# Attention scores with the bias on TensorE, attention steps in pairs, and offsets in a planner's order

## The chip, the cores and the metric

The kernel runs on one core of a Trainium2 chip. The metric is device microseconds from launch to end. A profile of one execution gives the time of every instruction on the engines: TensorE (PE, matmuls; PEld its weight loads), VectorE (DVE), ScalarE (ACT), GpSimd (POOL) and SyncE (SP), which issues the DMAs.

## The reference

For 4 batches, 8 heads, 768 positions and a head size of 64, each query attends to a window of its neighbours and to 24 block summaries of all keys. The result goes through a gated feed-forward network, whose weights come as float64.

```
k_sum = k.reshape(B, H, nb, 32, D).max(axis=3)       # block keys: maximum
v_sum = v.reshape(B, H, nb, 32, D).mean(axis=3)      # block values: mean
scores_l = where(|pos_q - pos_k| < 16, scale * q @ k.T, -1e9)
scores_s = scale * q @ k_sum.T + log(32)
a = exp(s - max(s));  a = a / (sum(a) + 1e-9)        # s: both kinds of scores side by side
x = a @ [v, v_sum]                                   # 3072 tokens x 512
g = x @ w_gate;  out = ((g * sigmoid(g)) * (x @ w_val)) @ w_out
```

## The kernel before, in words

**Attention.** A unit (k, u) is half a batch (384 tokens; k = 2 * batch + half) and a pair of heads u. There are 32 units, 8 to a batch. The tokens of a unit are cut into six groups of 64. A group's scores are 96 window columns and 24 block columns, 120 in all, and three groups share a PSUM bank. The steps of a unit are:

- SC (`a_scores`, L457): 24 matmuls of 64 x 64 weights by 120 columns, into two banks. The 120 columns come from a tile `kw` that holds, for each group, its window of keys and a copy of the block keys. For the first half of batch 0 `kw` is copied from the keys (`a_copy_windows`, L434), for all others it is loaded again from memory in 384-byte pieces (`a_load_windows`, L424). `join` (L449) puts the block keys behind them.
- `ttr` (`most`, L482): on VectorE, six instructions that take a bank's scores, add a bias (the mask and log 32), write them to SBUF and keep the minimum of the negated scores. Then six exps on ScalarE (L500), `eps` (L515), `rcp` (L518) and `nrm` (L521).
- PP0 and PP1 (L529): six transposes on TensorE, copied out as `pt`.
- XO (`a_out`, L550): 24 matmuls into one bank, then copied out by `xh` and `xl` (batch 0) or `xf`.
- The block values: `FV` in batch 0; in later batches a reduction `vpool`, a single transpose `PV` (`a_turn_values`, L651) and a copy `vs`.

**Network.** All of it runs as float32r with each operand split into a high and a low part, three products for one. `w_first` (L801) decodes a float64 weight tile on VectorE and ScalarE (`abs`, `clamp`, `shift`, `sign`, `low`), splits it (`hi`, `lo`), forms sums of quarters and stores them for the later batches. `o_first` (L839) does the same for each of the 12 tiles of the output weight, 512 wide. In batch 0 `u_plain` (L866) multiplies directly, 12 matmuls to a bank. In batches 1 to 3 `u_seven` (L911) uses seven products of quarters instead of eight, P1, P7, P5, P6, P2, P4, P3, in four banks, with VectorE adding them up (`vv`, `u2`, `c21`, `c12`, `c22`). `down` (L947) multiplies by the output weight and adds to `part`.

**Where the work stands in time.** While the network of one batch runs, the attention of the next is put between its steps (`units`, L1118). Batch 0's attention comes first, with batch 0's network behind it.

**What sets the order.** Nothing is ordered by hand. Every step is entered in a plan with an estimated time for each engine that could do it (`cost`, L74). `run` (L203) plays the plan through as a list scheduler: TensorE has a main line (the network) and a side line (attention), and takes of the two heads the one that can start first; other engines take the waiting step with the smallest due time. `order` (L170) does this three times, each time with due times from the round before, and sorts the steps by their planned start. The program is written in that order, so the order on each engine is fixed, and an instruction that waits holds up all that stand behind it on its engine. Where the plan has TensorE idle in the first 110 us, `warm_up` (L996) puts filler matmuls on a tile `warm`.

**Banks.** Of PSUM's eight banks three are a ring "t" (attention) and five a ring "m" (network; also some of batch 0's attention).

Of the kernel before, what the change touches and what calls it, by code (L numbers as in the profile page):

```python
# [18 lines left out]
DM = H * D  # L19
# [21 lines left out]

F64_LO = float(np.uint32(0x38000000).view(np.float32))
# [3 lines left out]
def score_bias() -> np.ndarray:  # L46

    m = np.zeros((P, 3, KC), np.float32)
    second, r = np.divmod(np.arange(P)[:, None], QT)
    c = np.arange(KW)[None, :]  # L50
    out = np.abs(r + WIN - c) >= WIN

    for v, edge in enumerate(((c < WIN) & (second == 0), c < 0, (c >= WIN + QT) & (second == 1))):
        m[:, v, :KW] = np.where(out | edge, np.float32(-1e9 / SCALE), np.float32(0))
    m[:, :, KW:] = np.float32(math.log(BLK) / SCALE)
    return m
# [46 lines left out]
class Step:  # L103
    def __init__(self, name, engines, do, n):
        self.name, self.engines, self.do, self.n = name, engines, do, n
        self.after, self.next = {}, []
        self.engine = self.start = self.end = None


class Plan:  # L110
# [26 lines left out]
    def add(self, name, engines, do, reads=(), writes=(), table=None, port=None):  # L137
# [3 lines left out]
        step.port = port  # L141
# [24 lines left out]
WAIT = 1.0  # L166
HOLD = 0.2


def order(steps):  # L170
# [13 lines left out]
    for _ in range(3):  # L184
# [18 lines left out]
def run(steps, line, late):  # L203
# [7 lines left out]
    table, place = None, [0, 0]  # L211
# [23 lines left out]
    while n:  # L235
        best = None
        for e, waiting in ready.items():
            if not waiting:
                continue
            if e == PE:  # L240
# [5 lines left out]
                s = min(heads, key=lambda s: (when(s), not s.side))  # L246
                pick = (when(s), 0, s)
# [35 lines left out]
        took = s.engines[e]  # L283
        if s.table and s.table != table:
            table, took = s.table, took + TABLE
# [5 lines left out]
        if e == PE:  # L291
            place[s.side] += 1
        n -= 1
# [4 lines left out]
def body(ctx, tc, qP, kP, vT, vP, wgv, wo, bias, ident, mean, out):  # L298
# [43 lines left out]
    def bank(which, name):  # L342
        return buf("psum", which, [P, 512], name, bufs={"t": 3, "m": 5}[which])
# [37 lines left out]
    bias_sb = buf("cst", "bias", [P, 3, KC], "bias_sb")  # L381
    id_sb = buf("cst", "id", [P, P], "id_sb")
    mean_sb = buf("pro", "mean", [P, NV, NB], "mean_sb")
# [9 lines left out]
    def a_keys(k, u):  # L393
        b = k // HALVES
        pool = "pro" if b == 0 and u % 2 else "att"
# [20 lines left out]
    def window_tile(k, u):  # L416
        if (k, u) not in KWD:
            pro = k == 0
            KWD[k, u] = buf(
                "pro" if pro else "att", f"kw{u}" if pro else "kw", [P, NT, KC], f"kw_{k}_{u}", bufs=1 if pro else 2  # L420
            )
        return KWD[k, u]
# [11 lines left out]
    def a_copy_windows(u):  # L434
        kt, kw = KT[0, u], window_tile(0, u)
        add_copy(
            f"winA({u})", (DVE, POOL, ACT), NT * QT, lambda: make(kw)[:, :, :QT],
            lambda: make(kt)[:, :TOK].rearrange("p (n j) -> p n j", j=QT), (kt,), ((kw, "w"),),
        )

        def tails():
            t = make(kt)
            return bass.AP(t.tensor, t.offset + QT, [t.ap[0], [QT, NT], [1, KW - QT]])

        add_copy(
            f"winB({u})", (DVE, POOL, ACT), NT * (KW - QT), lambda: make(kw)[:, :, QT:KW], tails, (kt,), ((kw, "v"),)
        )

# [7 lines left out]

    def a_scores(k, u):  # L457
        q, kw = Q[k, u], KWD[k, u]
# [3 lines left out]
        def do(e):  # L462
            warm_up(make(sc[0]))
            for i in range(NT):
                c, s = divmod(i, 2)
                qs = slice(i * QT, (i + 1) * QT)
                for h in range(2):
                    hs = slice(h * D, (h + 1) * D)
                    nc.tensor.matmul(  # L469
                        make(sc[h])[s * QT : (s + 1) * QT, c * KC : (c + 1) * KC], make(q)[hs, qs], make(kw)[hs, i, :],  # L470
                        start=True, stop=True,
                    )

        plan.add(f"SC({k},{u})", {PE: 0.95}, do, (q, kw), sc)

    def a_softmax(k, u):
# [20 lines left out]
        def half_exp(g):  # L497
            for c in range(NT // 2):
                i = g * NT // 2 + c
                nc.scalar.activation(  # L500
                    out=make(p)[:, i, :],
                    in_=make(p)[:, i, :],
                    func=AF.Exp,
                    scale=-1.0,
                    bias=make(nm)[:, i : i + 1],
                    accum_out=make(sm)[:, i : i + 1],
                )

        for g in range(2):
            plan.add(f"ttr{g}({k},{u})", {DVE: 1.1}, lambda e, g=g: most(g), (sc[g], bias_sb), ((p, g), (nm, g)))  # L510
        for g in range(2):
            plan.add(f"exp{g}({k},{u})", {ACT: 1.75}, lambda e, g=g: half_exp(g), ((nm, g),), ((p, g), (sm, g)), table="exp")
        plan.add(
            f"eps({k},{u})", {DVE: 0.18},
            lambda e: nc.vector.tensor_scalar(out=make(sm), in0=make(sm), scalar1=1e-9, scalar2=None, op0=ALU.add),  # L515
            (), (sm,),
        )
# [11 lines left out]
    def a_transposes(k, u):  # L529
        p = PR[k, u]  # L530
        if k == 0 and u % 2:
            pt = buf("pro", "pt", [KC, 2, TOK], f"pt_{k}_{u}")
        else:
            pt = buf("att", "pt", [KC, 2, TOK], f"pt_{k}_{u}")
        PT[k, u] = pt
        for g in range(2):
            pp = bank("m" if k == 0 else "t", f"pp{g}_{k}_{u}")

            def turn(e, g=g, pp=pp):
                warm_up(make(pp))  # L540
                for c in range(NT // 2):
                    nc.tensor.transpose(make(pp)[:KC, c * P : (c + 1) * P], make(p)[:, g * NT // 2 + c, :], make(id_sb))  # L542

            plan.add(f"PP{g}({k},{u})", {PE: 0.38}, turn, (p, id_sb), (pp,))
# [3 lines left out]
            )  # L548

    def a_out(k, u):  # L550
# [24 lines left out]
        plan.add(f"XO({k},{u})", {PE: 1.0}, do, reads, (xo,))  # L575
# [75 lines left out]
    def a_turn_values(b, u):  # L651
        vr = VR[b, u]
        pv = bank("t", f"pv_{b}_{u}")

        def do(e):
            nc.tensor.transpose(make(pv)[:NB, :P], make(vr), make(id_sb))

        plan.add(f"PV({b},{u})", {PE: 0.12}, do, (vr, id_sb), (pv,))
        if b not in VS:
# [4 lines left out]
            lambda e: nc.scalar.mul(make(vs)[KW:, u * P : (u + 1) * P], make(pv)[:NB, :P], 1.0 / BLK),  # L664
            (pv,), ((vs, u),),
# [173 lines left out]
    def o_first(j):  # L839
        raw = buf("wts", f"o{j}", [P, 2 * DM], f"raw_o{j}", I32)  # L840
        add_dma(f"raw_o{j}", P * DM * 8, lambda: make(raw), lambda: wo[j].bitcast(I32), (), (raw,))
        m = buf("dec", "mo", [P, DM], f"m_o{j}", bufs=2)
        decode(f"o{j}", raw, m, DM)
        w = O[j] = buf("wts", f"o{j}", [P, 2, DM], f"o{j}", F32R)
        split(f"o{j}", w, m, DM)
# [43 lines left out]
    def product(b, j, name, weight, xname, acc, first, last):  # L889
# [6 lines left out]
        def do(e):  # L896
            t = make(acc)
            warm_up(t)
# [12 lines left out]
    def u_seven(b, j):  # L911
        tmp = lambda name: buf("tmp", name, [P, TOK], f"{name}_{b}_{j}", room="tmp")
        p1, p7, p5, p6 = (bank("m", f"{x}_{b}_{j}") for x in ("p1", "p7", "p5", "p6"))
        of = lambda x: lambda: make(x)[:, :TOK]
        full = lambda x: lambda: make(x)
        product(b, j, "P1", "A11", "B11", p1, True, False)
        s1 = tmp("s1")
        add_copy(f"s1({b},{j})", (ACT, DVE), TOK, full(s1), of(p1), (p1,), (s1,), kind="evict")
        product(b, j, "P7", "S3", "T3", p7, True, False)
        s7 = tmp("s7")  # L920
        add_copy(f"s7({b},{j})", (ACT, DVE), TOK, full(s7), of(p7), (p7,), (s7,), kind="evict")
        product(b, j, "P5", "S1", "T1", p5, True, False)
        v = tmp("v")
        add_tt(f"vv({b},{j})", (DVE,), TOK, full(v), of(p5), full(s7), ALU.add, (p5, s7), (v,))
        product(b, j, "P6", "S2", "T2", p6, True, True)
# [21 lines left out]
    def down(b, g, t, spread):  # L947
# [6 lines left out]
        def piece(n):  # L954
            todo = pieces[n]

            def do(e):
                ps = make(acc)
                warm_up(ps)
                for j in todo:  # L960
                    ah, al = (make(x)[:, cs] for x in HH[b, j, hf])
                    wh, wl = (make(O[j])[:, x] for x in range(2))
# [5 lines left out]
            reads = sum(([*HH[b, j, hf], O[j]] for j in todo), [])  # L968
# [40 lines left out]
    def before_scores(k, u):  # L1009
# [4 lines left out]
        a_load_windows(k, u)  # L1014
# [4 lines left out]
        a_load_values(k, u)  # L1019
        a_join(k, u)  # L1020

    @aside
    def scores(k, u):
        before_scores(k, u)
        a_scores(k, u)
# [3 lines left out]
    def turned(k, u):  # L1029
        b, hf = divmod(k, HALVES)  # L1030
        if b and hf == 0:
            a_turn_values(b, u)
        a_values(k, u)
        a_transposes(k, u)

    @aside
    def result(k, u):
# [3 lines left out]
        else:  # L1041
            a_keep(k, u)

# [11 lines left out]
    def prepare(u):  # L1055
# [3 lines left out]
        a_copy_windows(u)  # L1059
        a_join(0, u)  # L1060

    for u in (1, 3):
        prepare(u)
        if u == 1:
            load_const(bias_sb, bias, P * 3 * KC * 4)
# [4 lines left out]
    load_const(id_sb, ident, P * P * 4)  # L1070
    load_first_values(0)

# [18 lines left out]
    plan.mark("late", "pro", lambda: (close_pool("pro"), open_pool("late", reuse_waits="tile")))  # L1091
# [9 lines left out]
    scores(1, 3)  # L1101
    for j in range(3):
# [15 lines left out]
    def units(b, at, gap, slack=SLACK):  # L1118
        plan.slack = slack
        for i in range(NP * HALVES):  # L1120
            k, u = b * HALVES + i // NP, i % NP
            todo.append((at + (i * gap / 2 if i < 2 else (i - 1) * gap), 2, lambda k=k, u=u: scores(k, u)))
            todo.append((at + (i + 0.55) * gap, 0, lambda k=k, u=u: turned(k, u)))
            todo.append((at + (i + 1) * gap, 1, lambda k=k, u=u: result(k, u)))
        todo.sort(key=lambda x: x[:2])
# [3 lines left out]
    def catch_up():  # L1129
        while todo and todo[0][0] <= clock[0]:  # L1130
            todo.pop(0)[2]()
# [7 lines left out]
    units(1, 0.0, 10.0, 1.5)  # L1139
# [12 lines left out]
    while todo:  # L1152
        todo.pop(0)[2]()
    for b in range(1, B):
        x_operands(b)
        clock[0] = 0.0
        if b + 1 < B:
            units(b + 1, 4.0, 14.5)
# [6 lines left out]
        while todo:  # L1165
            todo.pop(0)[2]()
# [56 lines left out]
```

## Time and profile before

| what | us |
|---|---|
| three runs | 696.02, 697.10, 697.63; median 697.1 |
| the profiled execution | 695.64 |
| its span, first to last instruction | 693.8 |
| TensorE busy | 676.6 (98%), 4918 matmuls |
| VectorE busy | 543.0 (78%) |
| ScalarE busy | 350.2 (50%) |
| GpSimd busy | 107.8 (16%) |

The span is what the profile sees of the execution; 1.8 us lie around it. Shares are of the whole span. They are averages over stretches with different limits, so a stretch has to be read by itself. Matmuls overlap in the pipeline: a matmul's own duration is longer than the distance to the next start, and it is that distance that counts.

### The profile page before, as it was taken

What the parts mean: (1) busy time and instruction counts of PE and PEld (TensorE: products, weight loads), DVE (VectorE), ACT (ScalarE), POOL (GpSimd) and SP (SyncE); (2) the same over time, 40 slices, a digit from 0 to 9 for tenths busy, and PEclk for the clock granted to TensorE, in tenths of its full rate; (3) what the DMA queues carried; (4) which work ended last, traced back from release to release, by engine and by line L of the source; (5) the groups of instructions that cost most, each with busy time, mean ns of one, the idle gap of its engine ahead of it and who ended that gap; (6) DMA issues with size and microseconds to landing.
All of it is one profiled execution on the core that took longest, in us unless ns stands there. A gap on an engine that the chain in (4) does not pass through costs nothing.

```text
span 693.8 us, 13084 instructions
## 1 busy us (share of the span) xinstructions
PE 676.6 (98%) x4918; PEld 612.9 (88%) x4918; DVE 543.0 (78%) x1296; ACT 350.2 (50%) x826; POOL 107.8 (16%) x115
## 2 busy tenths in 40 slices
PE   9797999999999999999999999999999999999997
PEld 8586899899799898989989898989989898989896
DVE  5889999989999898796878875696758862646464
ACT  4676655757666285655634375653734423212120
POOL 2344203031331320320101120000000200000000
PEclk9999999999999999999999999999999999999999
DMA  9999766766657698795847675583625553535322
GB/s 318 317 336 336 245 234 240 244 209 224 220 156 265 228 325 277 236 355 171 267 160 237 237 264 181 152 257 90 231 82 203 195 207 123 208 111 201 119 106 92
DMA packets 73327, 150.15 MB, mean 216 GB/s; under 512 B 25968, under 2 KB 48176, under 8 KB 67120
## 3 DMA queue, kind: packets, MB, share of 16 engines
q1 hardware_dynamic: 73264, 149.32, 63.4%
q8 instruction: 39, 0.64, 0.4%
q14 instruction: 24, 0.20, 0.1%
HBM read 114.70 MB, written 34.60 MB: 215 GB/s over the span
## 4 chain that ended last, share of the span: by engine, by line
PE 91%; DVE 5%; DMA 2%; ACT 1%; issue 1%; SPq 0%; ACTq 0%
PE p L904 39%; PE acc L964 28%; PE g L881 7%; PE v L881 7%; PE sc L469 3%; PE xo L573 3%; PE pp L542 2%; DMA q<-in_qP 2%; PE sc L999 1%; PE dummy L1006 1%; DVE w L354 1%; DVE pt L351 0%; ACT m_w L766 0%; DVE part L354 0%; DVE m_w L770 0%
## 5 line engine op out<-in xcount | busy, mean ns | idle before, releaser
L964 PE MATMUL acc<-o,hh 128*128 128x512 f32 x576 | 182.6, 398 | 0.0
L964 PEld LDWEIGHTS acc<-o,hh 128*128 128x128 f32 x576 | 104.7, 188 | 22.6 <-issue 1.4
L904 PE MATMUL p<-xh_T,s 128*128 128x384 f32 x432 | 120.2, 340 | 0.0
L964 PE MATMUL acc<-o,hl 128*128 128x512 f32 x288 | 112.8, 392 | 0.0
L904 PE MATMUL p<-xh_B,wa 128*128 128x384 f32 x288 | 86.8, 342 | 0.0
L500 ACT ACTIVATE p<-p,nm 128x120 f32<-128x120 f32 x192 | 73.5, 385 | 20.6 <-DVE nm L486 20.2
L904 PEld LDWEIGHTS p<-xh_T,s 128*128 128x128 f32 x432 | 78.9, 188 | 1.4 <-issue 0.3
L904 PE MATMUL p<-xl_T,s 128*128 128x384 f32 x216 | 72.4, 335 | 0.0
L354 DVE TENSOR_TENSOR part<-acc,part 128x512 f32<-128x512 f32 x72 | 48.5, 685 | 23.2 <-PE acc L964 22.8
L964 PEld LDWEIGHTS acc<-o,hl 128*128 128x128 f32 x288 | 54.1, 188 | 12.0 <-DVE hl L354 0.2
L881 PE MATMUL g<-xh_B,w 128*128 128x384 f32 x192 | 55.6, 350 | 5.0 <-DVE w L354 5.0
L354 DVE TENSOR_TENSOR c<-p,u 128x384 f32<-128x384 f32 x72 | 39.7, 553 | 22.7 <-PE p L904 22.5
L349 ACT COPY s<-p 128x384 f32<-128x384 f32 x52 | 24.9, 478 | 59.9 <-PE p L904 59.7
L349 ACT CAST hh<-a 128x384 fp32r<-128x384 f32 x53 | 27.1, 514 | 54.9 <-DVE a L354 53.8
L904 PEld LDWEIGHTS p<-xh_B,wa 128*128 128x128 f32 x288 | 53.1, 188 | 1.6 <-issue 1.0
L881 PE MATMUL v<-xh_B,w 128*128 128x384 f32 x192 | 53.8, 341 | 0.0
L354 DVE TENSOR_TENSOR hl<-a,hh 128x384 fp32r<-128x384 f32 x89 | 51.2, 578 | 2.9 <-ACT hh L349 0.5
L486 DVE CUSTOM_DVE_ANT_0 p<-sc,bias_sb 128x120 f32<-128x120 f32 x192 | 41.8, 275 | 10.0 <-PE sc L469 9.6
L904 PE MATMUL p<-xl_B,wa 128*128 128x384 f32 x144 | 48.3, 335 | 0.0
L354 DVE TENSOR_TENSOR v<-p,s 128x384 f32<-128x384 f32 x36 | 20.0, 557 | 34.0 <-PE p L904 33.3
L904 PE MATMUL p<-xh_T,wa 128*128 128x384 f32 x144 | 42.7, 337 | 0.0
L904 PE MATMUL p<-xh_B,s 128*128 128x384 f32 x144 | 42.5, 335 | 0.0
(124 smaller groups left out, 1365.0 us busy)
## 6 DMA issues: line engine op xcount, KB each, us to landing
wa<-wa SPq DMA_DIRECT2D x36, 768.0 KB, 4.3
s<-ss SPq DMA_DIRECT2D x24, 1024.0 KB, 7.5
raw_w<-in_wgv SPq DMA_DIRECT2D x12, 1024.0 KB, 6.2
ss<-s SPq DMA_DIRECT2D x12, 1024.0 KB, 4.9
wa<-w SPq DMA_DIRECT2D x12, 768.0 KB, 4.3
kw<-in_kP SPq DMA_DIRECT2D x28, 288.0 KB, 5.2
vw<-in_vP SPq DMA_DIRECT2D x28, 288.0 KB, 5.0
kt<-in_kP SPq DMA_DIRECT2D x16, 400.0 KB, 5.4
```

Of the source, the lines that this page charges most:

```text
L349: nc.scalar.copy(out, in_)
L354: vector[e].tensor_tensor(out=out, in0=a, in1=b, op=op)
L469: nc.tensor.matmul(make(sc[h])[s * QT : (s + 1) * QT, c * KC : (c + 1) * KC], make(q)[hs, qs], make(kw)[hs, i, :], start=True, stop=True,)
L486: nc.vector.tensor_tensor_reduce(out=make(p)[:, i, :], in0=make(sc[g])[:, c * KC : (c + 1) * KC], in1=make(bias_sb)[:, 0 if n == 0 else 2 ...
L500: nc.scalar.activation(out=make(p)[:, i, :], in_=make(p)[:, i, :], func=AF.Exp, scale=-1.0, bias=make(nm)[:, i : i + 1], accum_out=make(sm ...
L542: nc.tensor.transpose(make(pp)[:KC, c * P : (c + 1) * P], make(p)[:, g * NT // 2 + c, :], make(id_sb))
L573: nc.tensor.matmul(ps[hs, qs], v, make(pt)[:, h, qs], start=True, stop=True)
L881: nc.tensor.matmul(t[:, :TOK], a, x, start=u == 0 and n == 0, stop=u == NP - 1 and n == 2)
L904: nc.tensor.matmul(t[:, :TOK], a, x, start=first and kk == 0 and n == 0, stop=kk == 1 and n == 2, skip_group_check=not first,)
L964: nc.tensor.matmul(ps, a, w, start=j == js[0] and m == 0, stop=j == js[-1] and m == 2)
L999: nc.tensor.matmul(ps[:, TOK:], make(warm), make(warm), start=True, stop=True)
L1006: nc.tensor.matmul(make(first)[:, :P], make(warm), make(warm), start=True, stop=True)
```

## The change

1. **Bias on TensorE for batch 0** (k below 2). The bias, split into parts that float32r holds exactly, is a new input `parts`. SC of these units ends with 8 more matmuls of the identity by the bias, which add it in the bank. `ttr` gives way to one maximum over a bank (`max`) and a scaling of three numbers (`scl`). The exps read the bank and not SBUF. The mask's number becomes -2**33.
2. **Keys read in place for batch 0.** SC reads the 96 window columns from the keys' tile and the 24 block columns from `ks`, in two matmuls where there was one. The copies, the window loads and the joins of these 8 units go.
3. **Attention steps in pairs.** From batch 1 on `units` enters SC, SC; then PP of both; then XO, XO and the next SC, SC as a `burst`. Steps of a burst share the dependencies of its first, and `run` takes the next one of a burst if it can start within JOIN (0.35 us). Planned costs of SC and XO are changed, with extra time on a switch between kinds (`mode`).
4. **Banks** 4 and 4 for 3 and 5.
5. **Output weight in pairs**: `o_first` decodes two tiles at once, 1024 wide.
6. `PV` joins PP0 as a fourth transpose into the same bank. `u_seven` does P6 first from its second tile on, and `a_values` comes after the transposes.
7. **Exps one by one** in the plan where there were two steps of three; `eps` can go to ScalarE or GpSimd.
8. **Offsets.** `nudge` adds to the due times of 212 named steps a number from a table, or sets a slack, or pins the engine (13 to ScalarE, 24 to VectorE, 21 to GpSimd); then `run` plays the plan once more.

The diff, cut to its core:

```
+NUDGES = """
+kt(0,1) -60.2; id_sb -72.2; vr(1) -12.4; kt(0,0) +8.2; kt(0,2) +20.3; pool(0,2) +97.4; vn(0) +23.7; bias_sb +35.4
+scl1(0,3) -50.5 d; exp2(0,3) -108.4; exp5(0,3) -90; SC(0,0) s0.8; exp0(0,0) -54.7; exp1(0,0) -34.7; exp3(0,0) +137.8
...
+raw_w0 +14.7; low_w0 +106.4; wa0 +51.7; odd2(0) -51 p; val1(0) -42.4 p; odd2(2) -53.7 a; val1(2) -102.9 p
...
+exp3(1,3) +5.5; exp4(1,3) +47.8; eps(1,3) +121.7 p; raw_o0 +23.5; low_o0 +69.4; lo_o0 +58.3 d; raw_o2 +48.5
...
 def order(steps):
...
+    nudge(steps, late)
+    run(steps, line, late)
     return sorted(steps, key=lambda s: (s.start, s.n))
...
+    def burst(self, *makers):
+        n = len(self.steps)
+        for f in makers:
+            f()
+        lead, *others = [s for s in self.steps[n:] if PE in s.engines]
+        for s in others:
+            s.lead, s.slack = lead, 0.0
+            for o, whole in s.after.items():
+                if o.n < n:
+                    self.need(lead, o, whole)
...
+                for x in heads:
+                    if x.lead is not None and prior is not None and x.lead in (prior, prior.lead) and when(x) < free[PE] + JOIN:
+                        s = x
...
-        return buf("psum", which, [P, 512], name, bufs={"t": 3, "m": 5}[which])
+        return buf("psum", which, [P, 512], name, bufs={"t": 4, "m": 4}[which])
...
+                    if direct:
+                        x = hf * TOK + i * QT
+                        pieces = (0, make(keys[0])[hs, x : x + KW]), (KW, make(keys[1])[hs, :])
...
+            if biased:
+                for h in range(2):
+                    for c, n, v in ((0, 2, 0), (2, 1, 1)) if first else ((0, 1, 1), (1, 2, 1)):
+                        nc.tensor.matmul(
+                            make(sc[h])[:, c * KC : (c + n) * KC], make(id_r),
+                            make(parts_sb)[:, v * KC : (v + n) * KC], start=False, stop=True, skip_group_check=True,
+                        )
+                    for x in range(2):
+                        at = 3 * KC + x * NB
+                        nc.tensor.matmul(
+                            make(sc[h])[:, : 3 * KC].rearrange("p (n c) -> p n c", c=KC)[:, :, KW:], make(id_r),
+                            make(parts_sb)[:, at : at + NB].rearrange("p (o n) -> p o n", o=1).broadcast_to([P, 3, NB]),
+                            start=False, stop=True, skip_group_check=True,
+                        )
...
+        def greatest(g):
+            nc.vector.tensor_reduce(
+                out=make(nm)[:, g * 3 : g * 3 + 3], in_=make(sc[g])[:, : 3 * KC].rearrange("p (c k) -> p c k", k=KC),
+                axis=AX.X, op=ALU.max, negate=True,
+            )
...
+    def results_and_scores(some, more):
+        for k, u in more:
+            before_scores(k, u)
...
+        plan.burst(
+            *(lambda i=i: out(i) for i in range(2)),
+            *(lambda k=k, u=u: (a_scores(k, u), a_softmax(k, u)) for k, u in more),
+        )
...
-    units(1, 0.0, 10.0, 1.5)
+    units(1, 0.0, 20.0, 1.5)
...
-            units(b + 1, 4.0, 14.5)
+            units(b + 1, 4.0, 28.0)
```

## Rows read from the trace of the kernel before

**Rows 1.** Windows: busy us (x instructions) of each engine, PEclk, DMA share, GB/s.

```profile
0.00:40.00 40.00, 32.73 (x422) 28.77 (x423) 29.10 (x97) 21.34 (x69) 12.77 (x25) 1.00 0.96 318
40.00:105.00 65.00, 58.76 (x464) 53.77 (x464) 63.36 (x143) 43.93 (x98) 19.93 (x20) 0.97 0.84 281
105.00:235.00 130.00, 130.00 (x1006) 116.19 (x1005) 126.09 (x293) 81.60 (x188) 39.00 (x35) 1.00 0.65 219
235.00:690.00 455.00, 455.00 (x3031) 414.13 (x3030) 323.63 (x765) 203.30 (x473) 36.09 (x36) 1.00 0.58 198
```

**Rows 2.** Window 0 to 105 us, TensorE's matmuls on `warm` alone.

```profile
0.00:105.00 105.00, 23.80 (x170) 0.98 0.89 295
```

**Rows 3.** Chain of the first 100 us: its shares by line, then start us, us, what.

```profile
by line: DMA q<-in_qP 12.6%; PE g L881 12.5%; PE v L881 10.4%; issue 5.8%; PE sc L999 4.7%; PE dummy L1006 4.5%; DVE w L354 4.4%; PE sc L469 4.1%; DVE pt L351 2.5%; ACT m_w L766 2.2%; DVE m_w L770 2.0%; DVE p L521 2.0%; DVE m_w L783 1.9%; D
...
59.42 3.90 PE g L881 x12
63.32 2.08 PE v L881 x12
```

**Rows 4.** Timeline of TensorE, a lone XO and SC: start us, us, instruction.

```profile
282.75 0.34 PE L904 MATMUL p<-xh_B,wa 128*128 128x384 f32 x1
283.01 0.92 PE L573 MATMUL xo<-pt,vw 120*64 120x64 f32 x24
283.86 0.44 PE L904 MATMUL p<-xh_T,s 128*128 128x384 f32 x1
284.14 0.34 PE L904 MATMUL p<-xl_T,s 128*128 128x384 f32 x1
...
286.15 0.85 PE L469 MATMUL sc<-kw,q 64*64 64x120 f32 x24
286.92 0.45 PE L904 MATMUL p<-xh_T,s 128*128 128x384 f32 x1
```

**Rows 5.** Timeline of TensorE, XO followed by SC.

```profile
66.65 0.92 PE L573 MATMUL xo<-pt,vw 120*64 120x64 f32 x24
67.50 0.85 PE L469 MATMUL sc<-kw,q 64*64 64x120 f32 x24
68.28 0.45 PE L881 MATMUL g<-xh_B,w 128*128 128x384 f32 x1
```

**Rows 6.** Lines L469 and L573: duration ns min/median/max, first and last start.

```profile
L469 PE MATMUL sc<-kw,q x768: 262/263/314, 7.7 to 513.1; 64*64 64x120 f32 x192
...
L573 PE MATMUL xo<-pt,vw x720: 222/222/271, 23.5 to 540.5; 120*64 120x64 f32 x180
```

**Rows 7.** Groups of VectorE, 0 to 235 us: busy us, mean ns | idle before.

```profile
L486 DVE CUSTOM_DVE_ANT_0 p<-sc,bias_sb 128x120 f32<-128x120 f32 x96 | 20.7, 273 | 0.2 <-DMA bias_sb<-in_bias 0.2
L783 DVE SCALAR_TENSOR_TENSOR m_w<-raw_w,m_w 128x1024 int32<-128x1024 int32 x12 | 17.3, 1438 | 0.0
...
L783 DVE SCALAR_TENSOR_TENSOR m_o<-raw_o,m_o 128x512 int32<-128x512 int32 x12 | 9.2, 775 | 0.0
...
L404 DVE TENSOR_REDUCE ks<-kt 128x24 f32<-128x768 f32 x9 | 8.5, 947 | 3.9 <-DMA kt<-in_kP 3.9
L770 DVE TENSOR_SCALAR m_w<-m_w 128x1024 f32<-128x1024 f32 x12 | 8.2, 684 | 1.3 <-ACT m_w L766 1.2
...
L770 DVE TENSOR_SCALAR m_o<-m_o 128x512 f32<-128x512 f32 x12 | 5.0, 426 | 0.0
...
L515 DVE TENSOR_SCALAR sm<-sm 128x6 f32<-128x6 f32 x16 | 3.7, 229 | 0.2 <-ACT p L500 0.2
...
L351 DVE COPY kw<-ks 128x144 f32<-128x144 f32 x6 | 1.8, 303 | 0.1
```

**Rows 8.** The page's groups: busy us, mean ns | idle before, and its releaser.

```profile
L354 DVE TENSOR_TENSOR c<-p,u 128x384 f32<-128x384 f32 x72 | 39.7, 553 | 22.7 <-PE p L904 22.5
```

**Rows 9.** Tile `xl_B` on GpSimd: duration ns min/median/max, first and last start.

```profile
L354 POOL TENSOR_TENSOR xl_B<-xf,xh_B x5: 1011/1332/5533, 222.6 to 540.2; 128x384 fp32r<-128x384 f32 x5
```

**Rows 10.** Line L500 on ScalarE, the exps: duration ns min/median/max.

```profile
L500 ACT ACTIVATE p<-p,nm x192: 377/382/400, 14.1 to 518.2; 128x120 f32<-128x120 f32 x192
```

More of the change, by code (lines that the diff above doesn't have):

```diff
@@ L53, in score_bias, with bias_parts @@
     for v, edge in enumerate(((c < WIN) & (second == 0), c < 0, (c >= WIN + QT) & (second == 1))):
-        m[:, v, :KW] = np.where(out | edge, np.float32(-1e9 / SCALE), np.float32(0))
+        m[:, v, :KW] = np.where(out | edge, np.float32(MASK), np.float32(0))
     m[:, :, KW:] = np.float32(math.log(BLK) / SCALE)
+    return m
+def bias_parts() -> np.ndarray:
+    m = np.zeros((P, 3 * KC + 2 * NB), np.float32)
+    first = m[:, : 3 * KC].reshape(P, 3, KC)
+    first[:] = score_bias()
+    x = np.float32(math.log(BLK) / SCALE)
+    for to in (first[:, :, KW:], m[:, 3 * KC : 3 * KC + NB], m[:, 3 * KC + NB :]):
+        part = (x.view(np.uint32) & np.uint32(0xFFFF0000)).view(np.float32)
+        to[:] = part
+        x = np.float32(x - part)
     return m
@@ new lines, with nudge @@
+mul(1,0,1) +58.9 p; pool(2,0) +48.2; vpool(2,0) -58.2; q(4,1) +111.3; kw(4,1) +48.8; pool(2,1) +43.5
+vpool(2,1) +49.5; vw(4,1) +27.4; exp3(4,0) -52.3; ttr1(4,1) -8.9; eps(4,1) -38.4 a; sl(1) -54.9 p; s1(1,1) -3.1 d
+vv(1,1) -37.2; mul(1,1,0) -38.8; c22(1,1) +85.3 d; pool(2,2) -145.4; pool(2,3) -132.1; ls(1,3) +8.5
+"""
+def nudge(steps, late):
+    by = {s.name.replace(" ", "_"): s for s in steps}
+    for line in NUDGES.replace("\n", ";").split(";"):
+        if not line.strip():
+            continue
+        name, *what = line.split()
+        s = by[name]
+        for x in what:
+            if x[0] in "+-":
+                late[s] += float(x)
+            elif x[0] == "s":
+                s.slack = float(x[1:])
+            else:
+                s.engines = {x: s.engines[x]}
@@ L283, in run @@
         took = s.engines[e]
+        if e == PE and prior is not None and (s.mode or "f") != (prior.mode or "f"):
+            took += 0.1 if s.mode else 0.19
+        elif e == PE and prior is not None and not s.side and prior.side:
+            took += 0.09
         if s.table and s.table != table:
@@ L297, in body @@
 @with_exitstack
-def body(ctx, tc, qP, kP, vT, vP, wgv, wo, bias, ident, mean, out):
+def body(ctx, tc, qP, kP, vT, vP, wgv, wo, bias, parts, ident, mean, out):
     nc = tc.nc
@@ L432, in a_load_windows @@
         )
[L434 to L447, printed above, removed]
     def a_join(k, u):
@@ L455, in a_join, with on_bank @@
         )
+    def on_bank(k, u):
+        return k < HALVES
     def a_scores(k, u):
-        q, kw = Q[k, u], KWD[k, u]
+        q = Q[k, u]
+        direct = k < HALVES
+        hf = k % HALVES
+        keys = [KT[0, u], KS[0, u]] if direct else [KWD[k, u]]
+        biased = on_bank(k, u)
+        first = k % HALVES == 0
         which = "m" if k == 0 and u % 2 else "t"
@@ L511, in a_softmax, with one_exp @@
-        for g in range(2):
[L512 to L517, printed above, removed]
+        def one_exp(i):
+            nc.scalar.activation(
+                out=make(p)[:, i, :],
+                in_=make(p)[:, i, :],
+                func=AF.Exp,
+                scale=-1.0,
+                bias=make(nm)[:, i : i + 1],
+                accum_out=make(sm)[:, i : i + 1],
+            )
@@ L649, in a_pool_values, with a_keep_values @@
         plan.add(f"vpool({b},{u})", {DVE: 0.95}, do, (vt,), (vr,), port=False)
[L651 to L658, printed above, removed]
+    def a_keep_values(b, u, pp):
         if b not in VS:
@@ L966, in do @@
                         )
-            reads = sum(([*HH[b, j, hf], O[j]] for j in todo), [])
+            reads = sum(([*HH[b, j, hf], O[j][0]] for j in todo), [])
             plan.add(f"D{n}({b},{g},{t})", {PE: 0.229 * 3 * len(todo)}, do, reads, (acc,))
@@ L1119, in units @@
         plan.slack = slack
[L1120 to L1125, printed above, removed]
+        every = [(b * HALVES + i // NP, i % NP) for i in range(NP * HALVES)]
+        pairs = [every[i : i + 2] for i in range(0, len(every), 2)] + [[]]
+        todo.append((at, lambda: scores_of_pair(pairs[0])))
+        for i in range(len(pairs) - 1):
+            todo.append((at + (i + 0.55) * gap, lambda i=i: turned_pair(pairs[i])))
+            todo.append((at + (i + 1) * gap, lambda i=i: results_and_scores(pairs[i], pairs[i + 1])))
     clock = [0.0]
```

222 lines of the change are left out of this document (153 added, 69 removed).

## The prediction

> **What bounds the kernel now.** I read the busy time by stage first [rows 1]. From 105 to 690 us TensorE is busy in every microsecond (130.00 of 130, 455.00 of 455). VectorE is nearly full as well up to 235 us (63.36 of 65, then 126.09 of 130), and has room after it (323.63 of 455). Up to 105 us TensorE is busy for 32.73 + 58.76 of 105, so it idles 13.5 us, and 23.80 us of what is busy are the filler matmuls on `warm`, which compute nothing [rows 2]. So there are three stretches with three limits:
>
> - 0 to 105 us: TensorE has 13.5 + 23.8 = 37.3 us without useful work. The chain of waits has 12.6 of its first 100 us on loads [rows 3].
> - 105 to 235 us: TensorE and VectorE are full together. Here the rest of the batch-0 work (weight decoding) and batch 1's attention lie.
> - 235 to 690 us: TensorE alone. A microsecond of TensorE taken away there is a microsecond of the total.
>
> After 690 us there are 4 us of tail that the change doesn't touch. The profiled execution took 695.64 us, 1.46 less than the median of the runs, 697.1; the sum is made against 695.64 and then raised by 1.5.
>
> **Part 1: steps of attention in pairs (`burst`).** TensorE's order is read in the timeline. Matmuls of the main stream start 0.17 us apart (12 in 2.08 us [rows 3]). Before a lone XO step the distance is 0.26 (282.75 to 283.01), so going in costs 0.09; XO lasts 0.85 to the next start; the first matmul after it takes 0.28 (283.86 to 284.14), so coming out costs 0.11. A lone SC lasts 0.77 and is entered and left in the same way [rows 4]. In one place XO is followed by SC directly: XO 0.85, SC 0.78, with no extra between [rows 5]. So joining unlike steps saves one way in and one way out, 0.20. Joining like steps saves the last gap too: an SC matmul lasts 0.263 and the group's 0.85 us end at 287.00, so its last one starts at 286.74, 0.18 before the stream goes on; for XO 0.15 in the same way (0.92 and 0.222) [rows 4, 6]. That is 0.38 for SC after SC, 0.35 for XO after XO. No pair of like units stands unstalled in the trace, so the bounds for a like join are 0.20 (the unlike one) and 0.38.
>
> A batch of 8 units makes one burst SC SC, three of XO XO SC SC and one XO XO: 0.38 + 3 x (0.35 + 0.20 + 0.38) + 0.35 = 3.5 us. A join fails when the second step isn't ready within JOIN, and the fourth step of a burst needs banks that the first two XO have just filled (there are four "t" banks), so part of it comes back as a wait. I take two thirds, 2.3 us a batch. Batches 2 and 3 have their units between 235 and 540 us, where TensorE is the only limit: **-4.5 us** (0 to -7.0). Batch 1's share falls where VectorE is full too and counts as nothing; if VectorE gets enough room there it is 2.3 more. Transposes gain nothing.
>
> **Part 2: VectorE in the first 235 us** [rows 7]. The trace has 16 units there, 8 of them batch 0's.
> - `wo` in pairs: two 512-wide STT of 775 become one of 1438 (0.11 saved), two tensor-scalar of 426 one of 684 (0.17). The other two decode steps are of the same two kinds; I take them at half. 0.42 per pair, six pairs: -2.5 us (-1.7 to -3.4).
> - Joins of batch 0 go, since keys are read in place: VectorE did 6 joins of 303 ns here; taken at 1.3 us.
> - The 96 minima take 20.7 us, 0.216 each, so batch 0's 48 take 10.3. In their place come 16 maxima over 3 x 120 elements read from the bank and 16 tiny scalings. The nearest row is a reduction of 768 elements in 947 ns: in proportion to elements 0.44, and at most 0.95. I take 0.55, nearer the proportion: 8.8. Scalings: `sm` with 6 elements takes 0.229; half on ScalarE: 1.8. Sum 10.6 for 10.3: +0.3 (-3.2 to +8.6).
> - `eps` may go to ScalarE or GpSimd: 16 x 0.229 = 3.7; half of them, -1.8 (0 to -3.7).
>
> Sum **-5.3 us**. VectorE is 94 to 97% busy there, so it counts nearly in full as long as it stays the limit.
>
> **Part 3: the start.** Four window loads of batch 0's second half go (128 x 6 x 96 x 4 B = 295 KB each, 1.18 MB), at 281 to 318 GB/s [rows 1] 3.7 to 4.2 us of a queue that is 84 to 96% full. A 0.21 MB load is added ahead of the first scores, 0.7 us, with two copies. The offsets also put early `wo` loads later. The chain holds 12.6 us of waiting on loads [rows 3]; I take **-2 us** (+1.4, two such loads' worth of delay on the first chain, to -12.6). The other offsets reorder what VectorE and ScalarE do: VectorE idles 235 - 29.10 - 63.36 - 126.09 = 16.5 us before 235 us, which is all that a better order could bring; I take **-1**. Part of that is the clock: granted 0.97 from 40 to 105 us and 1.00 in all other stretches [rows 1]. At 59.42 us, after waiting for a decoded weight, TensorE took 3.90 us for 12 matmuls that take 2.08 at 63.32 [rows 3], so it ran there at the lower of its levels, 1.2 GHz; 1.8 us return if that wait goes.
>
> **Part 4: what TensorE gets in addition.** Bias: per unit 2 x (240 + 120 + 72 + 72) = 1008 columns; a 384-column matmul takes 0.17 [rows 3], so 0.45 us. Keys in place: 24 more, shorter matmuls; between 0 and the 0.78 that the present 24 take, taken at 0.2 because they are a fifth as wide. Over 8 units 5.2 us (3.6 to 9.8), all before 105 us or just behind, beside the 37.3 us in which TensorE has nothing to do. Costed at nothing; with the cover gone, +5.2.
>
> **Part 5: banks 3 + 5 become 4 + 4.** With four main banks, the bank that `c12` reads is taken two products later (P6, then P1: 2.1 us). After 235 us VectorE reads such banks in 553 ns and mostly stood idle waiting for them (22.5 us over 72) [rows 8], so the bank is free in time; where VectorE has a backlog it isn't. **+1.0 us** (0 to +5).
>
> Where the pins put VectorE's work on GpSimd, the trace shows a price: one subtraction took 1.01 us at best and 5.53 at worst on GpSimd, VectorE being busy beside it [rows 9]. The Trainium skill (SBUF — State Buffer, section "SBUF: two separate sides") says that VectorE and GpSimd take a shared port pair as an exclusive lock and the loser blocks entirely. By that rule the work pinned to GpSimd (21 pins) comes back as blocked time; the trace's spread speaks for it, and it is the third case below.
>
> **Sum:** -4.5 - 5.3 - 2 - 1 + 0 + 1 = -11.8; 695.6 - 11.8 = 683.8, and with 1.5 for the median **685.3 us**.
>
> **The rivals.**
> - *The order does much more:* the offsets fill most of VectorE's 16.5 us and take most of the 12.6 us of load waits; 10 us beyond my 3: 675. For it: the chain's early pieces are waits, not work [rows 3]. Against: VectorE has only 1.6 us idle from 40 to 105 [rows 1]; the rest would have to come from its first 40 us, where it waits for the first loads.
> - *GpSimd blocks VectorE:* the eps, join and start terms vanish (-1.8, -1.3, -3); left are -4.5 - 2.5 + 0.3 + 1: 691.4. For it: the 5.53 us above. Against: GpSimd is busy in only 71.7 of 235 us [rows 1].
> - *It doesn't do what it says:* the pairs don't come to stand side by side, as the planner takes a main step when a second step is not ready, and the start is as before: the parts lost, about 696.5 to 697.
> - *Slower, by score banks held longer:* in batch 0 the exps now read the bank, which was free after six minima (1.3 us) and now waits for six exps at 382 ns [rows 10], 2.3, and for whatever ScalarE has in front of them; with an abs and a cast of some 1 us each in between, 3.3 us longer a unit. TensorE's order is fixed, so a unit that waits for a bank holds the main steps behind it, and these hold weights and decoding. Six units (four of the second half, two of the first) with a full stall: 20 us; it decides from 12 us on, where it eats the sum. At 20 us: 705. For it: ScalarE is busy 43.93 of 65 us there [rows 1]. Against: those stalls fall first on the 37.3 us without work.
>
> **How the numbers follow.** No change means within 0.2%, 1.4 us, which is what repeated runs of this kernel can tell. Forecast (680 to 690) 0.55; the order does more (670 to 680) 0.17; GpSimd blocks (690 to 695.5) 0.13; nothing (695.7 to 698.5) 0.05; slower 0.10. Faster 0.55 + 0.17 + 0.13 = 0.85, same 0.05, slower 0.10. Range 676 to 697: it leaves out about half of the second case below and most of the slower one above, under 2 in 10; the bounds of the maxima (+8.3 beyond my value) and of the banks (+4) together stay inside it.
>
> **What would show it.** In the profile after: SC and XO groups of 48 matmuls between 235 and 540 us, and the last batches shorter by about 2 us each (TensorE has no idle time there before, so its stretch shortens); the point where TensorE goes gapless earlier than 105 us, and the filler plus idle time down by about 5 more than what bias and keys add; VectorE's busy time before the end of batch 0's work down by about 5 us; a maximum at 0.5 to 0.6 us. Wrong would be: TensorE waits longer than 0.3 us for a bank after 235 us, GpSimd instructions of several us beside stalled VectorE ones, or SC matmuls before 105 us waiting on ScalarE's exps.

## The result, and the profile after

The changed kernel takes 687.49 us (median of five, 687.26 to 690.92) against 697.63; the ratio is 0.9859, 95% interval 0.9843 to 0.9876. The forecast was 685.3, its range 676 to 697. The total came out as forecast; what it is made of did not, as the experiments show.

The profile read here is that of another execution (`after_again`, 685.0 us of span), since the one that came with the result was the slowest of five, and that of before was a quick one, so that the profiles lie 8.8 us apart and the medians 10.1. The stretches are cut where the network of a batch begins with its first seven-product matmul. First the kernel before, then the changed one. Columns as in [rows 1].

```profile
0.00:234.64 234.64, 221.13 (x1887) 198.37 (x1887) 218.19 (x530) 146.87 (x353) 71.70 (x79) 0.99 0.75 253
234.64:393.85 159.21, 159.21 (x1158) 143.34 (x1157) 132.57 (x325) 86.60 (x205) 25.10 (x23) 1.00 0.77 258
393.85:553.05 159.20, 159.20 (x1157) 143.34 (x1156) 116.43 (x304) 84.65 (x202) 10.99 (x13) 1.00 0.54 182
553.05:693.76 140.71, 137.02 (x721) 127.80 (x719) 75.80 (x140) 32.05 (x66) 0.00 (x0) 1.00 0.41 148
```

```profile
0.00:230.74 230.74, 224.84 (x2125) 207.09 (x2125) 202.75 (x406) 153.83 (x366) 69.08 (x74) 0.99 0.76 263
230.74:387.12 156.38, 156.07 (x1157) 144.15 (x1156) 126.46 (x307) 83.58 (x213) 18.64 (x22) 1.00 0.74 247
387.12:542.45 155.33, 155.33 (x1158) 144.16 (x1156) 111.20 (x291) 81.45 (x210) 9.85 (x13) 1.00 0.55 186
542.45:684.98 142.53, 137.64 (x721) 127.75 (x719) 75.37 (x140) 32.92 (x66) 0.00 (x0) 1.00 0.41 146
```

The second number of a row is its length. The four stretches change by -3.9, -2.8, -3.9 and +1.8 us, -8.8 in all. In the first stretch VectorE (third busy column) does 15.4 us less, and the stretch is only 3.9 shorter. The last batch, which the forecast left alone, is longer.

The joins, in the timeline of TensorE after, answering to [rows 4, 5]:

```profile
300.72 0.39 PE L1108 MATMUL acc<-o,hl 128*128 128x512 f32 x1
301.04 1.62 PE L710 MATMUL xo<-pt,vw 120*64 120x64 f32 x48
302.59 1.49 PE L561 MATMUL sc<-kw,q 64*64 64x120 f32 x48
304.01 0.72 PE L1108 MATMUL acc<-o,hh 128*128 128x512 f32 x2
```

Four steps take 2.97 us from 301.04 to 304.01, where 2 x (0.85 + 0.77) = 3.24 were needed alone, and are entered and left once and not four times (3 x 0.20). 0.87 us are saved, where the forecast's bounds for like joins gave up to 0.93: two XO take 1.55 for 1.70, as forecast, and two SC 1.42 for 1.54, so SC's last gap is worth 0.12 and not 0.18. The groups are whole: 48 and 48.

The new steps, VectorE's groups up to 230.74 us in the same profile, answering to [rows 7]:

```profile
L592 DVE CUSTOM_DVE_ANT_0 p<-sc,bias_sb 128x120 f32<-128x120 f32 x48 | 10.5, 275 | 0.5 <-PE sc L561 0.4
L614 DVE TENSOR_REDUCE nm<-sc 128x3 f32<-128x360 f32 x16 | 8.0, 523 | 4.9 <-PE sc L574 4.8
L913 DVE SCALAR_TENSOR_TENSOR m_o<-raw_o,m_o 128x1024 int32<-128x1024 int32 x6 | 7.3, 1216 | 0.0
...
L444 DVE COPY pt<-pp 120x384 f32<-120x384 f32 x6 | 3.2, 550 | 0.0
...
L624 DVE TENSOR_SCALAR nm<-nm 128x3 f32<-128x3 f32 x7 | 1.0, 162 | 0.1
```

A maximum takes 0.52 us (0.55 was assumed). The copies `pt` fell from 21 to 6 on VectorE; ScalarE took the others.

A unit's SC with its bias (start of its first matmul, and of the first matmul after it):

```profile
64.28 0.41 PE L561 MATMUL sc<-kt,q 64*64 64x96 f32 x8
...
66.22 0.42 PE L1014 MATMUL g<-xh_B,w 128*128 128x384 f32 x1
```

That is 1.94 us, where a unit's SC took 0.78 before [rows 5].

### The profile page after: what moved, and what is told of

The parts are those of the page before. It is cut to its first block, busy times and chain, and to the rows that moved or that the text cites. A ratio compares the mean times of both kernels' runs of the same rounds, so it can differ in the third digit from the quotient of the medians.

```text
span 689.1 us, 13426 instructions
## 1 busy us (share of the span) xinstructions
PE 673.0 (98%) x5156; PEld 621.2 (90%) x5156; DVE 515.4 (75%) x1141; ACT 352.0 (51%) x855; POOL 96.8 (14%) x109
## 4 chain that ended last, share of the span: by engine, by line
PE 75%; DMA 10%; DVE 10%; issue 2%; ACT 2%; POOL 1%; SPq 1%; ACTq 0%; POOLq 0%; DVEq 0%
PE p L1038 32%; PE acc L1108 25%; PE g L1014 5%; DMA s<-ss 4%; PE v L1014 4%; PE xo L710 3%; PE sc L561 2%; PE pp L677 2%; DMA sf<-m_w 2%; DMA kt<-in_kP 1%; DVE m_w L919 1%; DVE m_w L913 1%; DMA vt<-in_vT 1%; POOL m_w L447 1%; DMA wa<-wa 1%
## 5 line engine op out<-in xcount | busy, mean ns | idle before, releaser
L1108 PE MATMUL acc<-o,hh 128*128 128x512 f32 x576 | 179.4, 392 | 0.6 <-DVE o L447 0.6
L1108 PEld LDWEIGHTS acc<-o,hh 128*128 128x128 f32 x576 | 107.1, 188 | 23.2 <-DVE o L447 0.9
L1038 PE MATMUL p<-xh_T,s 128*128 128x384 f32 x432 | 122.8, 339 | 1.8 <-DMA s<-ss 1.3
L1038 PE MATMUL p<-xh_B,wa 128*128 128x384 f32 x288 | 84.8, 335 | 0.0
L442 ACT COPY s<-p 128x384 f32<-128x384 f32 x64 | 30.8, 481 | 102.8 <-PE p L1038 102.8
L1014 PE MATMUL g<-xh_B,w 128*128 128x384 f32 x192 | 53.9, 341 | 3.2 <-DVE w L447 1.7
L604 ACT ACTIVATE p<-p,nm 128x120 f32<-128x120 f32 x144 | 55.1, 384 | 1.1 <-DVE nm L592 0.6
L447 DVE TENSOR_TENSOR a<-c,a 128x384 f32<-128x384 f32 x69 | 39.8, 580 | 4.7 <-ACT a L996 2.1
L1038 PEld LDWEIGHTS p<-xl_T,s 128*128 128x128 f32 x216 | 40.6, 188 | 0.3
```

Source lines behind the costliest of these rows:

```text
L442: nc.scalar.copy(out, in_)
L447: vector[e].tensor_tensor(out=out, in0=a, in1=b, op=op)
L604: nc.scalar.activation(out=make(p)[:, i, :], in_=make(p)[:, i, :], func=AF.Exp, scale=-1.0, bias=make(nm)[:, i : i + 1], accum_out=make(sm ...
L1014: nc.tensor.matmul(t[:, :TOK], a, x, start=u == 0 and n == 0, stop=u == NP - 1 and n == 2)
L1038: nc.tensor.matmul(t[:, :TOK], a, x, start=first and kk == 0 and n == 0, stop=kk == 1 and n == 2, skip_group_check=not first,)
L1108: nc.tensor.matmul(ps, a, w, start=j == js[0] and m == 0, stop=j == js[-1] and m == 2)
```

## The experiments

Times are medians; "the partner" is the kernel before on the same chip. Each edit is against the changed kernel unless it says otherwise.

**after_again, after_five: the change once more.** No edit.

> The changed kernel as it is, profiled once more, because its profiled execution (690.92 us) was the slowest of five and 3.4 us above their median. If that execution was an odd one: span near 685.5 us, with the first stretch (up to the first seven-product matmul) or the one of batch 1 shorter than the 230.8 and 159.1 us seen, and the four waits of the last batch for the load of s (0.5 to 0.9 us each) still there. If the profile always costs 3 us: 690 to 691 again.

687.05 us (0.9851, 0.9834 to 0.9868), span 685.0. The stretch of batch 1's network was 159.1 us in the first profile and is 156.4 here. The waits of the last batch are there in both. As partner of the last run below:

> The changed kernel, as the partner of the next one on the same chip: 687 us.

688.27 us (0.9860, 0.9834 to 0.9885).

**no_offsets: the table emptied.**

```
-NUDGES = """ ... 212 entries ... """
+NUDGES = ""
```

> The table of offsets emptied, all else as in the changed kernel. My theory (the offsets gain little, the pairs and VectorE's relief carry it): 688 to 691 us, 1 to 3 us slower than with them, the loss before 235 us. Rival (the offsets are the main part): 694 us or more, with TensorE's time without useful work before 105 us back near 37 us and VectorE near 97% busy up to 235 us.

701.44 us, ratio 1.0055 (1.0034 to 1.0076). My theory fell. Without the table the change is slower than the kernel before, so the table is worth 14 us. Its stretches:

```profile
0.00:240.17 240.17, 227.94 (x2147) 210.81 (x2147) 215.77 (x433) 153.19 (x360) 48.28 (x57) 0.99 0.72 252
240.17:401.54 161.37, 158.76 (x1157) 145.40 (x1156) 125.99 (x312) 83.49 (x211) 16.17 (x17) 0.99 0.72 241
401.54:556.87 155.33, 155.33 (x1157) 144.16 (x1156) 111.14 (x291) 81.44 (x210) 9.86 (x13) 1.00 0.56 186
556.87:698.11 141.24, 137.40 (x721) 127.74 (x719) 75.48 (x140) 32.92 (x66) 0.00 (x0) 1.00 0.41 148
```

The offsets give 9.4 us in the first stretch and 5.0 in the second, nothing in the third, where TensorE has no gap either way; in the last they cost 1.3. Up to batch 1 they took 13.0 us off VectorE and put 20.8 on GpSimd (48.28 to 69.08). The filler matmuls on `warm`, without the table and then with it:

```profile
0.00:105.00 105.00, 24.58 (x174) 0.97 0.76 268
```

```profile
0.00:105.00 105.00, 21.18 (x152) 0.98 0.81 287
```

All fillers stand before 105 us. So TensorE's first stretch is made of idle time, fillers and the rest: 13.5, 23.8 and 197.3 us before [rows 2]; 12.2, 24.6 and 203.4 without the table; 5.9, 21.2 and 203.7 with it. The rival's sign came out: some 37 us without useful work both before and without the table, 27 with it. Its other sign did not, as VectorE is busy for 90% of the stretch and not 97. What TensorE waits for, without them and then with them (us in total, times, longest):

```profile
PE pp L644 <- DVE p L623: 6.8, 3, 3.3
PE p L1005 <- DVE s L414: 2.0, 1, 2.0
PE g L981 <- DVE w L414: 2.0, 2, 1.7
```

```profile
PE pp L677 <- DVE p L656: 2.1, 2, 1.6
...
PE g L1014 <- DVE w L447: 1.0, 2, 0.8
```

Transposes stood 6.8 us before normalised scores that VectorE's queue brought late, and 2.1 with the offsets. One of these waits, without the table, in the timeline of VectorE and TensorE:

```profile
87.41 0.95 DVE L749 TENSOR_REDUCE vr<-vt 128x24 f32<-128x768 f32 x1 [2.32 <-DMA vt<-in_vT]
88.28 0.18 DVE L620 RECIPROCAL ri<-sm 128x6 f32<-128x6 f32 x1
88.38 0.65 DVE L873 TENSOR_SCALAR m_o<-m_o 128x1024 int32<-128x1024 int32 x1
88.95 0.90 DVE L623 TENSOR_TENSOR p<-p,ri 128x720 f32<-128x720 f32 x1
...
89.91 1.53 PE L644 MATMUL pp<-id_sb,p 128*120 128x128 f32 x6 [2.94 <-DVE p L623]
```

VectorE was not too busy here: it stood idle for 2.32 us, as the reduction `vr` of the next batch was first in its order and its load had not landed. The reciprocal and the product that TensorE waited for stood behind it. TensorE's clock adds to such waits:

```profile
89.80:93.20 3.40, 3.29 (x31) 3.07 (x32) 3.18 (x4) 0.96 (x2) 0.00 (x0) 0.50 0.37 112
298.00:301.40 3.40, 3.40 (x12) 3.40 (x12) 2.51 (x6) 0.00 (x0) 0.00 (x0) 0.50 0.95 328
```

From about the end of the wait of 2.94 us, and soon after the one of 2.0 us (which ended at 297.54), the granted clock is 0.50, the lower level of 1.2 GHz, for 3.4 us each. Both places are at the full clock with the table, so an estimate from these rows, half of 3.4 us for each, puts at most 3.4 of the 14 us down to the clock. A third such place, at 35 us, has its like with the table, at 33.

**pins_only, offsets_early: which part of the table.** The first keeps the pins and the slacks, the second the first 75 entries.

```
             if x[0] in "+-":
-                late[s] += float(x)
+                pass
```

> The pinned engines and the slacks of the table kept, all due-time offsets out. Theory (the table moved some 15 us of VectorE's work before 235 us to GpSimd and ScalarE, and that is its gain): 688 to 694 us, VectorE at about 230 us of work in the first stretch against 245 without the table. Rival (the gain is in which load and which step comes first): 698 us or more.

> Only the first 75 entries of the table, those of the start (up to the third weight tile). Theory (most of the 14 us is the start's, 9 us of it seen in the first stretch): 690 to 694 us, the point from which TensorE has no gaps back near 82 us and the first stretch near 232 us. Rival (the entries only work together): 697 us or more.

696.31 us (0.9974, 0.9957 to 0.9990) and 698.81 (1.0019, 1.0004 to 1.0035): 5.1 and 2.6 of the 14.4 us. Neither theory holds as put; the rival of `offsets_early` does. The first stretch with the pins alone:

```profile
0.00:235.22 235.22, 225.43 (x2133) 207.61 (x2133) 215.69 (x424) 150.67 (x357) 60.38 (x69) 0.99 0.74 256
```

The pins put 12.1 us more on GpSimd than there is without the table and left VectorE at 215.7 us, so what VectorE does less in the changed kernel is a result of pins and due times together; the early entries alone brought the first stretch to 238.8 us, not 232. The table works as a whole.

**plain_no_joins: no offsets, steps of a pair not tied; no_joins: the same with the offsets.**

```
         for f in makers:
             f()
+        return
```

> No offsets and no joins, to be compared with the run that has no offsets but has joins (701.4 us). Theory (a joined burst saves 0.9 us, some 3 us a batch, also without offsets): 707 to 711 us, the stretches of batches 1 and 2 about 3 us longer each. Rival (the 12 us by which the run with offsets but without joins was slower than no offsets at all came from offsets that fit another order, and joins save little): 700 to 704 us.

> The steps of a pair are entered as before but no longer tied together, so the planner takes them as they come; offsets kept. Theory (joined XO and SC steps save 0.9 us for each XO XO SC SC, about 3 us a batch, of which batches 2 and 3 count in full): 6 to 8 us slower than with joins, 693 to 696 us, with SC and XO groups of 24 in the timeline after 235 us. Rival (the gain came from VectorE's relief before 235 us): at most 3 us slower, 688 to 690 us.

717.48 us (1.0280, 1.0254 to 1.0305) against 701.44 with joins; with the offsets 713.78 (1.0231, 1.0209 to 1.0253) against 687.05. Both lie past what theory and rival expected. In the third stretch, in which TensorE has no gap (no offsets, no joins):

```profile
413.62:572.67 159.05, 159.05 (x1157) 143.29 (x1156) 107.58 (x288) 83.33 (x210) 9.45 (x15) 1.00 0.52 182
```

159.05 against 155.33: the joins save 3.7 us a batch (159.04 with the offsets). The rest of the difference lies mostly before it (the first stretch 251.1 against 240.2 us), and that is more than their price on TensorE: units are entered in pairs here, and run singly. The largest piece of it is one wait, again of order:

```profile
PE acc L1076 <- ACT a L964: 4.9, 1, 4.9
```

ScalarE had the twelve exps of a pair of units in front of the `a` that TensorE's next step was waiting for, and the granted clock fell to the lower level within that wait, from 190.5 to 197.4 us. The wait, some 2 us for the clock (half of the 4.05 that TensorE was busy in that time) and 3.7 for the joins of batch 1's units, which stand in this stretch too, make an estimate of 10.6 of the 10.9 us. The offsets, made for an order with joins, help by only 3.7 us here.

**plain_no_bias: no offsets, the bias on VectorE again, keys still in place.**

```
     def on_bank(k, u):
-        return k < HALVES
+        return False
```

> No offsets, and batch 0's bias on VectorE again (the six minima of before), keys still read in place; to be compared with 701.4 us. Theory (the bias costs TensorE 1.15 us a unit, 9 us in all, but TensorE has more than that without work before 105 us): 700 to 703 us. Rival (the added TensorE work lies on the chain of the start and is why the start without offsets is 5.5 us longer than before): 694 to 698 us, the first stretch back at 232 to 236 us.

702.07 us (1.0065, 1.0041 to 1.0088) against 701.44. Without the table, moving the bias to TensorE cost nothing clear of noise, and gained nothing. But TensorE did not simply have the time to spare: with the bias taken off it, its first stretch was 242.45 us, with 14.4 idle and 27.4 of fillers, and the granted clock at the lower level for 17.0 us, against 6.8 in `no_offsets`. The work left, and other waits came in its place.

**before_o_pairs: the kernel before, with the output weight in pairs (and no fillers in the second piece of a down step).**

```
+        if j % 2:
+            return
-        m = buf("dec", "mo", [P, DM], f"m_o{j}", bufs=2)
+        m = buf("dec", "mo", [P, 2 * DM], f"m_o{j}")
```

> The kernel before with the output weight decoded in pairs and nothing else (and the fillers left out of the second piece of a down step). Theory (4.1 us less VectorE work before 235 us, where VectorE is the limit): 693 to 696 us, all of it in the first stretch. Rival (VectorE's relief alone buys nothing, since its order and the due times of the fourth tile, decoded earlier than needed, set the start): 697 to 701 us.

700.59 us (1.0034, 1.0016 to 1.0052). The rival's forecast holds: relief of VectorE in this form buys nothing. A pair also comes as one larger load, and its first tile later, which this run can't tell from the relief. First stretch:

```profile
0.00:238.39 238.39, 223.60 (x1886) 199.61 (x1887) 215.77 (x508) 151.53 (x349) 60.16 (x70) 0.99 0.76 257
```

VectorE does 2.4 us less and the stretch is 3.8 us longer; it now idles 22.6 us there against 16.5. TensorE waits 6.0 us for decoded weights, 5.0 before. Not all of the 3.8 is the edit's: around the longest of these waits the granted clock is at the lower level for 6.8 us here and 3.4 in the profile of before,

```profile
59.20:66.00 6.80, 5.89 (x18) 5.89 (x19) 6.16 (x12) 5.16 (x15) 1.12 (x1) 0.50 1.02 419
```

```profile
59.40:62.80 3.40, 3.38 (x11) 3.38 (x12) 3.40 (x10) 1.55 (x8) 3.20 (x3) 0.50 0.95 331
```

which is some 1.3 us (half of 5.89 - 3.38). The medians are 1.9 us apart.

**before_4_4: the kernel before, with banks 4 and 4 alone.**

```
-        return buf("psum", which, [P, 512], name, bufs={"t": 3, "m": 5}[which])
+        return buf("psum", which, [P, 512], name, bufs={"t": 4, "m": 4}[which])
```

> The kernel before with its banks split 4 and 4 and nothing else. Theory (the bank that c12 reads is free within two products in nearly all places, so the price is small): within 2 us of before, 696 to 700 us, the stretch of the last batch longer by at most 1 us. Rival (five main banks were needed): 703 us or more, with waits of TensorE for VectorE's reads in the seven-product stretches.

700.62 us (1.0033, 1.0015 to 1.0051), 1.9 us slower by the medians, 2.3 by the ratio. The seven-product stretches are the same within 0.4 us (159.61, 159.17, and 141.03 in the last batch); the price is in the first, 237.87, where the lower clock again lasts 6.8 us and not 3.4.

**p1_first: P1 before P6; p1_first_five: the same in five rounds.** In the last batch of the changed kernel, TensorE's P6 waits (first profile of it, the matmul before the wait and after it):

```profile
559.95 0.34 PE L1038 MATMUL p<-xh_B,s 128*128 128x384 f32 x1
...
560.83 0.44 PE L1038 MATMUL p<-xh_T,s 128*128 128x384 f32 x1 [0.54 <-DMA s<-ss]
```

```
-        if j:
-            one("P6", "S2", "T2", True)
         one("P1", "A11", "B11", False)
+        if j:
+            one("P6", "S2", "T2", True)
```

> P1 before P6 in the later weight tiles, so that the load of wa is asked for first and s one product (1.05 us) later. Theory (P6 first asks for s before it has landed; in the last batch s lands at 560.79 us and TensorE goes on at 560.83): the four waits of the last batch go, 2.8 us, and perhaps 1 us in batches 1 and 2: 683.5 to 685 us. Rival (the waits are for a bank of the ring of four): they stay, 687 to 688 us, as the ring only turns by one.

> The changed kernel with P1 before P6, in five rounds, since three left the intervals overlapping (685.78 against 687.05 us). Theory (the waits for the load of s are real, 1.9 us in the last batch and some 0.6 in batch 1): 1.2 to 2.5 us faster than its partner. Rival (chance): within 0.7 us of it.

685.78 us (0.9838, 0.9817 to 0.9859), just past the theory's 685, then 685.32 (0.9807, 0.9782 to 0.9832) against its partner's 0.9860, with every run (684.60 to 686.39) below every run of the changed kernel on that chip (from 688.13). Its last batch:

```profile
542.23:682.82 140.59, 136.75 (x721) 127.82 (x719) 72.69 (x132) 36.55 (x74) 0.00 (x0) 1.00 0.41 148
```

140.59, against 142.53 with P6 first and 140.71 before the change, and no seven-product matmul waits any more. The wait was for the load of `s`, which P6 asks for at the start of a tile, where P1 asks for `wa`; a bank would have waited either way. A wait costs more than the idle time in brackets: 559.95 and 560.83 are 0.88 us apart, where the stream has 0.17. Without the table P6 is first too, and the last batch took 141.24, so when the load lands depends on the order ahead of it. This version beats both kernels.

## Why the prediction was right, and which of its steps were not

The sum was -11.8 us and the profiles give -8.8 (the medians -10.1). That the total came out is luck in good part, as its steps show:

- **Joins, -4.5.** The mechanism and the 0.9 us of a burst are right. The third that was taken off for joins that fail was not lost: every burst from batch 2's units on stood whole, 3.9 us in the third stretch, 3.7 of them the joins'. Together with the second stretch -6.7; why that one gave 1.1 us less is shown only in part (with P1 first it is 155.9 us long and not 156.4).
- **VectorE's relief counts nearly in full, -5.3.** This step failed. Sizes of single steps were right (a maximum 0.52 for 0.55; with the decoding in pairs VectorE did 2.4 us less, for 2.5). But without the table the whole change took only 2.4 off VectorE in the first stretch, and VectorE's busy share was taken for a limit, which it was not. At 215.7 to 215.8 us of VectorE's work the first stretch took 235.2 us (`pins_only`), 238.4 (`before_o_pairs`) and 240.2 (`no_offsets`), and 234.6 before at 218.2. The rows at 87.41 us show how: what TensorE needs stands in VectorE's order behind a step that waits itself.
- **Offsets, -1, and the start, -2.** Mis-sized by far: 14.4 us between `no_offsets` and the change. The bound that the forecast named, VectorE's idle time, was not used up (it grew from 16.5 to 28.0 us); the bound that mattered was TensorE's 37.3 us without useful work, of which the table took 10. It did so with another order and with 20.8 us more on GpSimd; the runs don't tell the two apart. The 1.8 us of the clock did not come back: the 5.0 us wait that ended at 59.42 is gone, but behind a wait of 1.6 us, which ended at 32.62, the clock is at the lower level from 32.6 to 36.0. The rival that let the order do much more had the cause, though not the total, since what the order adds is needed to make up for the slower start.
- **Bias and keys on TensorE, nothing.** The size was too small: a unit's SC takes 1.94 us for 0.78, which is 9.3 us over 8 units where 5.2 was taken. That it costs nothing did not hold by itself: without the table the 37 us that were to cover it stayed, and TensorE's other time in the first stretch grew by 6.0 us, about the 5.5 by which the stretch is longer. (The 9.3 less some 3 us for the joins of batch 1's units comes to that.) With the table the cover was used. Taking the bias alone off again did not bring the start back, so the bias by itself isn't shown to be the cause.
- **Banks, +1.** Mis-sized, and not where it was looked for: 1.9 us by itself, in the first stretch. Beside it stands +1.8 in the last batch, a step that the forecast did not have: P6 first asks for a load before it has landed.
- **GpSimd blocks VectorE.** The blocking is there, its price is not. (The table pins 33 steps to VectorE and 28 to GpSimd, more than the 24 and 21 that stand in the list of the change.) In `after_again`:

```profile
177.82 2.39 POOL L447 TENSOR_TENSOR o<-m_o,o 128x1024 fp32r<-128x1024 f32 x1 [4.05 <-ACT o L442]
178.19 2.44 DVE L447 TENSOR_TENSOR hl<-a,hh 128x384 fp32r<-128x384 f32 x1 [0.96 <-ACT hh L442]
```

VectorE's subtraction takes 0.51 us at best; this one ends 0.4 us after GpSimd's is through, and a second one, at 205.26, took 2.29 in the same way. But these two are the only ones of its size that took over 2 us in the first stretch, and with 20.8 us more on GpSimd than without the table the stretch is 9.4 us shorter. GpSimd's `xl_B` took 1.44 us at worst, for 5.53 [rows 9].

- **It doesn't do what it says.** It does: the pairs stand side by side.
- **Slower, by banks held for the exps.** TensorE's waits for ScalarE's exps came to 0.5 us. Without the table the change was slower, but no wait for an exp shows there: TensorE waits for normalised scores and decoded weights.

The total was right because errors cancelled: relief that buys nothing and added work that was not free, against offsets worth much more.

## What to carry to other kernels

A nearly full engine beside an idle one is not yet the limit: ask which of its instructions the other waits for, and whether less work brings that one forward. In a list-scheduled program the order, with the engines that steps are put on, is a term by itself; here it was larger than all the edits, and offsets fitted to one order are worth little in another. Idle time on an engine covers added work only if the order lets it. When a step moves to the front of its loop, look up when its load lands.

## What the runs showed of the hardware

Going from the full-size float32r stream into 64-row steps and back costs TensorE 0.20 us, and going from XO to SC within a burst nothing that shows (302.59 - 301.04 = 1.55 for two XO, where two alone take 1.70). The exps that read PSUM took 362 ns each on ScalarE, those from SBUF 383 (means of 48 each, first stretch of `after_again`). A VectorE subtraction that started 0.37 us into a GpSimd one took 2.44 us where 0.51 is the least. Around the end of some waits of 1.6 to 5.0 us TensorE's granted clock was at the lower level, for 3.4 us or for 6.8; behind others, as the one of 2.1 us that ended at 18.81 us before, it stayed at the upper.
